# Four row chunks of x at the start of a gated pair of linear-attention blocks: two turned by transposing transfers in place of TensorE, and A's key and query weights loaded from ScalarE's queue

## The chip, the cores and the metric

The kernel runs on 1 core of one Trainium2 chip. The metric is the device time of one execution in microseconds (us), the median over several runs; lower is better.

## What is computed

x is 2048 x 640 (one batch), in bf16. Two linear-attention blocks, A and B, read the same x with their own weights, and a gate mixes their outputs.

```python
def block(x, wqkv, wo):                    # H = 32 heads, Dh = 20
    q, k, v = heads(x @ wqkv)
    phi = lambda t: jnp.where(t > 0, t + 1, jnp.exp(t)) + 1e-6
    pq, pk = phi(q), phi(k)
    kv = jnp.einsum("bhsd,bhse->bhde", pk, v)
    z  = jnp.einsum("bhsd->bhd", pk)
    o  = jnp.einsum("bhqd,bhde->bhqe", pq, kv) / (pq . z + 1e-6)
    return merge(o) @ wo

g = sigmoid((x * gate_w).sum(-1))
out = g * block(x, A_wqkv, A_wo) + (1 - g) * block(x, B_wqkv, B_wo)
```

## The kernel before

**Layout.** Rows of x are worked on in 16 chunks of 128 (four blocks of 512). x is held twice in SBUF: `xn`, rows on the partitions, and `xT`, the 640 columns on the partitions in five pieces `c` of 128. A product x @ W takes a piece of `xT` as the stationary operand and streams W (keys, `kA`, 128 x 320 per half `hf`), or takes W as the stationary operand and streams 512 rows of `xT` (queries, `qA`, `q`). Behind the products ScalarE takes an exponential out of PSUM (`e`) and VectorE clamps it and takes a maximum; results are `pk` (keys) and `pqTA`, `pqTB` (queries). Many of the products are written in a Strassen-like form with sums made on VectorE (`SQ`, `TQ` in `MB` and `TM`). Two hand-written lists of step names, `FIRST` and `PLAN`, set the order of all of that; the change touches neither.

**The start.** The four chunks 0 to 3 (the first 512 rows) come into `xn` by four plain loads (`load_x`, L200): chunks 0 and 1 are called x0 and x1 below. They go through TensorE transposes into PSUM and VectorE copies into `xT` (`x_transpose`, L290 to L296). The other three blocks of 512 rows are turned by 15 transposing transfers on SyncE's queue (L220, 128 columns x 512 rows each). A's key weights `wkA` come in four loads (L203): pieces c = 0, c = 1, c = 2 and c = 3 with 4, called wk0, wk1, wk2 and wk34 here. A's query weights `wqA` come in three (L217): pieces 0 and 1, 2 and 3, and 4, called wq01, wq23 and wq4 here.

TensorE begins with seven warm-up matmuls on constants (`warm`, L252), then turns chunks 0 and 1, and turns the gate's weight vector into a column (`gate_column`, L263 to L268). ScalarE copies that column into `wkA` as its 641st column, in three pieces (L268). Every key matmul of the second half of the columns (`hf` = 1, 321 wide) reads it, so the x @ gate_w sum comes for free. `k_first` (L359) writes out the order of the 40 key matmuls of the chunks 0 to 3, which are 8 (chunks 0 and 1, c = 0 and 1: the four of the first half, then the four of the second), and 32 more with the transposes of the chunks 2 and 3 between them. Then `FIRST` goes on with the first query products (`E.P1` at L753, `sq`/`tq` sums on VectorE, `E.P2`), and the key chunks 4 to 15.

**What orders transfers.** The order of the instructions on each engine is the order of the program text. ScalarE (ACT) and SyncE (SP) each issue transfers on a queue of their own, between their other instructions, and an instruction with a wait holds all that stand behind it on its engine. The tile framework deals out eight completion semaphores to the transfers, one after another in the program's order, both queues together (`DMAHW0` to `DMAHW7`). The ninth transfer takes the semaphore of an earlier one, and waits, on the queue that issues it, until the transfer that had it last has landed. So in the printed instruction order `[waits DMAHW0_49]` on a transfer is a wait for an earlier transfer, often of other data and of the other queue.

Of the kernel before, what the change touches and what calls it, by code (L numbers as in the profile page):

```python
# [9 lines left out]
P = 128  # L10
# [5 lines left out]
S, D, H = 2048, 640, 32  # L16
Dh = D // H
DT = D // P
ST = S // P
NB = 4  # L20
CB = 4
HB = 512
# [56 lines left out]
def kernel(  # L79
# [11 lines left out]
    nc = tc.nc  # L91
    x2 = A_x.flatten_outer_dims()
# [28 lines left out]
    def ps_raw(name, slot=None):  # L121

        if slot is None:
            slot = turn[0]
            turn[0] = (slot + 1) % 4
        return pools.get(slot, pools["ps"]).tile([P, 4 * HB], BF16, tag=f"ps{slot}", name=name)

    def banks(raw):

        return raw.bitcast(FP32).rearrange("p (b n) -> p b n", b=2)  # L130

    def ps(name, slot=None):

        return banks(ps_raw(name, slot))

    xT = persist.tile([P, DT, S], BF16, name="xT")
    xn = persist.tile([P, ST, D], BF16, name="xn")
# [17 lines left out]
    g5 = persist.tile([DT, P], BF16, name="g5")  # L155
# [29 lines left out]
    wq_dram = [A_wqkv.rearrange("(c p) f -> p c f", p=P), B_wqkv.rearrange("(c p) f -> p c f", p=P)]  # L185
# [5 lines left out]
    nc.vector.memset(tiny[:], LOGS * EPS)  # L191
    nc.vector.memset(maskE[:], 1.0)
    nc.vector.memset(E4[0:2 * H, HF:D], 0.0)
    xb0 = x2[0:CB * P, :].rearrange("(p q) d -> p q d", q=CB)
    wk = [None, None]
    wv = [None, None]
    wq = [None, None]
    wk[0] = wpool.tile([P, DT, D + 2], BF16, tag="wk", name="wkA")
    def load_x(eng, lo, hi):
        eng.dma_start(out=xn[:, lo:hi, :], in_=xb0[:, lo:hi, :])  # L200

    def load_wk(eng, lo, hi):
        eng.dma_start(out=wk[0][:, lo:hi, 0:D], in_=wq_dram[0][:, lo:hi, D:2 * D])  # L203

    load_x(nc.sync, 0, 1)
    load_x(nc.scalar, 1, 2)
    load_wk(nc.sync, 0, 1)
    load_wk(nc.scalar, 1, 2)
    nc.sync.dma_start(out=g5[:], in_=gate_w.rearrange("(c p) -> c p", p=P))
    load_x(nc.scalar, 2, 3)  # L210
    load_wk(nc.sync, 2, 3)
    load_x(nc.scalar, 3, 4)
    nc.scalar.preload_act_table_set("natural_log_exp_and_others")
    load_wk(nc.sync, 3, DT)
    wq[0] = wpool.tile([P, DT, D], BF16, tag="wq", name="wqA")
    for lo, hi in ((0, 2), (2, 4), (4, DT)):
        nc.sync.dma_start(out=wq[0][:, lo:hi, :], in_=wq_dram[0][:, lo:hi, 0:D])  # L217
    for n in range(1, NB):
        for c in range(DT):
            nc.sync.dma_start_transpose(  # L220
                out=xT[:, c, n * HB:(n + 1) * HB], in_=x2[n * HB:(n + 1) * HB, c * P:(c + 1) * P]
            )


    make_identity(nc, ident[:])
    for r in range(4):
        rows = slice(32 * r, 32 * r + 32)
        nc.gpsimd.tensor_copy(out=I4[rows], in_=ident[rows, rows])
    nc.gpsimd.tensor_copy(
        out=spread[:].rearrange("p (h t) -> p h t", t=TW), in_=I4[:, :, None].to_broadcast([P, H, TW])  # L230
    )
    for lo in range(0, HF, K6):
        part = maskE[:, lo:min(lo + K6, HF)]
        for sign, base in ((1, 0), (-1, Dh - 1)):
            nc.gpsimd.affine_select(
                out=part, in_=part, pattern=[[-sign * Dh, part.shape[1] // Dh], [0, Dh]],
# [3 lines left out]
    for rows, n in ((slice(0, 2 * H), H // 2), (slice(2 * H, P), H)):  # L240
        nc.gpsimd.tensor_copy(
            out=E4_rows[rows, 0:n], in_=I4[rows, 0:n, None].to_broadcast([rows.stop - rows.start, n, Dh])
# [20 lines left out]
    def gate_column(pt):  # L263

        at = slice(4 * HB - 2 * P, 4 * HB - 2 * P + DT)
        nc.tensor.transpose(out=pt[:, at], in_=g5[:], identity=ident[0:DT, 0:DT])
        for lo, hi in ((0, 1), (1, 2), (2, DT)):
            nc.scalar.copy(out=wk[0][:, lo:hi, D:D + 1], in_=pt[:, at, None][:, lo:hi])  # L268
# [21 lines left out]
    def x_transpose(i, slot):  # L290
        pt = ps_raw("xt", slot)
        for c in range(DT):
            nc.tensor.transpose(out=pt[:, c * P:(c + 1) * P], in_=xn[:, i, c * P:(c + 1) * P], identity=ident[:])
        src = pt[:, 0:D].rearrange("p (c n) -> p c n", c=DT)
        for lo, hi in ((0, 2), (2, DT)):
            nc.vector.tensor_copy(out=xT[:, lo:hi, i * P:(i + 1) * P], in_=src[:, lo:hi])  # L296
# [39 lines left out]
    def k_mm(b, i, c, pt, hf):  # L336
        n = HF + (b == 0 and hf == 1)
        nc.tensor.matmul(  # L338
            pt[:, hf, 0:n], lhsT=xT[:, c, i * P:(i + 1) * P], rhs=wk[b][:, c, hf * HF:hf * HF + n],
            start=(c == 0), stop=(c == DT - 1),  # L340
        )
# [17 lines left out]
    def k_first():  # L359

        pts = []

        def part(i, cs, hfs=(0, 1)):
            for c in cs:
                for hf in hfs:
                    k_mm(0, i, c, pts[i], hf)

        x_transpose(0, 3)
        x_transpose(1, 2)
        gate_column(warm_raw)  # L370
        pts += [ps("kA", 1), ps("kA", 3)]
        for hf in range(2):
            for i in range(2):
                part(i, (0, 1), (hf,))
        x_transpose(2, 0)
        for i in range(2):
            part(i, (2,))
        x_transpose(3, 2)
        pts.append(ps("kA", 0))
        part(2, (0, 1, 2))  # L380
        for i in range(3):
            part(i, (3, 4))
        pts.append(ps("kA", 2))
        for hf in range(2):
            part(3, range(DT), (hf,))
        return pts

    def mixed(t, m):
# [146 lines left out]
    class PhiSteps:  # L535
# [9 lines left out]
        def part(self, t, k):  # L545
            return t if len(self.srcs) == 1 else t[:, k]
# [573 lines left out]
    def rows_of(i):  # L1120
        n, q = divmod(i, CB)
        rows = out2[n * HB:(n + 1) * HB, :]
        return rows.rearrange("(p q) d -> q p d", q=CB)[q] if n == 0 else rows[q * P:(q + 1) * P, :]

    def prod(dst, left, right, i, first, cs=range(DT)):

# [12 lines left out]
    class Pair:  # L1139
# [7 lines left out]
        def store(self, k, lo=0, hi=D):  # L1147
            eng = nc.scalar if self.last and k == 1 else nc.sync
            eng.dma_start(out=rows_of(self.i + k * (ST // 2))[:, lo:hi], in_=self.osb[k][:, lo:hi])
# [163 lines left out]

    with tc.manual_schedule():
        pts = k_first()
        for n in range(1, NB):
            nc.sync.dma_start(
                out=xn[:, n * CB:(n + 1) * CB, :], in_=x2[n * HB:(n + 1) * HB, :].rearrange("(q p) d -> p q d", p=P)
            )
# [3 lines left out]
        lo, hi = GT  # L1323
# [197 lines left out]
        part = [slice(n * RB, (n + 1) * RB) for n in range(4)]  # L1521
# [70 lines left out]
        for i in range(1, half):  # L1592
            p, after = pairs[i], pairs[i + 1] if i + 1 < half else None
# [7 lines left out]
            q = after if i + 2 < half else p if after is None else None  # L1601
# [42 lines left out]
```

## Time and profile before

| what | value |
|---|---|
| median of 3 runs | 181.88 us (181.76 to 182.73) |
| the profiled execution, its own time | 182.31 us |
| its span in the profile | 180.5 us |
| busy: TensorE, VectorE, ScalarE | 176.9, 152.0, 112.0 us |
| transposing transfers on SyncE's queue | 15, issued from 5.80 us on |
| first query matmul (L753) | 11.64 us |

The profiled execution's own time is 1.8 us over its span, which is what lies around the span, and 0.43 us over the median of the runs. Times in the profile count from the start of the span. In the rows of the timeline the first number is a start, the second the length to the end of the last instruction of a merged group; "x8" is how many were merged; brackets give idle time ahead of it and what ended that. ACTq and SPq are the issuing of transfers by ScalarE and SyncE; PE is TensorE's matmuls, PEld its weight loads, DVE VectorE.

### The profile page before, as it was taken

The page shows a single profiled execution, that of the slowest core. Times are in us where ns is not written, and L with a number is a line of the kernel's source. Part 1 is how long each engine was busy: PE and PEld are TensorE (multiplying, and loading weights), DVE is VectorE, ACT ScalarE, POOL GpSimd, SP SyncE. Part 2 cuts the span into 40 slices and gives each one's busy share as a digit, 9 for nine tenths or more (in the row PEclk, how much of TensorE's full clock was granted, in tenths as well). Part 3 has the DMA queues.
Part 4 walks back from the last instruction along what each step waited for, and adds up shares of the span by engine and source line. Part 5 has one row for each costly group of instructions (what it writes and reads, how often), then busy time and mean ns, then how long its engine had stood idle before and what let it go on. Part 6 is the DMA issues. An engine that isn't in the chain of part 4 may idle for free.

```text
span 180.5 us, 3397 instructions
## 1 busy us (share of the span) xinstructions
PE 176.9 (98%) x1276; PEld 117.6 (65%) x1276; DVE 152.0 (84%) x287; ACT 112.0 (62%) x235; POOL 4.4 (2%) x19
## 2 busy tenths in 40 slices
PE   8999999999999999999999999999999999999993
PEld 3666666665666677666656676766678777777772
DVE  1479999999999996888899997987988988686774
ACT  2098988999763434587778686774815756456410
POOL 7100000000000000000000000000000000000000
PEclk9999999999999999999999999999999999999999
DMA  5995449976035015000000024144901560133123
GB/s 184 284 187 91 97 106 291 356 158 182 0 112 185 8 54 181 2 0 0 2 4 2 0 32 153 31 127 123 264 3 48 167 153 0 40 137 119 73 101 120
DMA packets 21602, 18.85 MB, mean 104 GB/s; under 512 B 9298, under 2 KB 21074, under 8 KB 21586
## 3 DMA queue, kind: packets, MB, share of 16 engines
q1 hardware_dynamic: 20722, 17.82, 35.3%
q10 hardware_dynamic: 864, 0.82, 1.3%
q8 instruction: 10, 0.16, 0.4%
q14 instruction: 6, 0.05, 0.1%
HBM read 11.86 MB, written 4.80 MB: 92 GB/s over the span
## 4 chain that ended last, share of the span: by engine, by line
PE 96%; ACT 2%; DVE 1%; issue 0%
PE q L527 16%; PE kA L338 11%; PE kB L338 9%; PE gs L845 9%; PE gs L1333 9%; PE oy L1129 6%; PE oz L1129 5%; PE ox L1129 5%; PE ow L1129 4%; PE kB L527 3%; PE qA L393 3%; PE gB L815 2%; PE gA L815 2%; PE warm L252 2%; ACT e L551 1%; PE q L393 1%
## 5 line engine op out<-in xcount | busy, mean ns | idle before, releaser
L338 PEld LDWEIGHTS <-xT 128*128 128x128 bf16 x280 | 27.3, 98 | 15.1 <-DVE xT L296 0.2
L338 PE MATMUL kA<-wkA,xT 128*128 128x320 bf16 (+1 forms) x160 | 24.8, 304 | 0.0
L551 ACT ACTIVATE e<-q 128x512 bf16<-128x512 f32 x32 | 18.5, 599 | 5.7 <-PE q L527 5.2
L557 DVE TENSOR_SCALAR e<-e 128x640 bf16<-128x640 bf16 (+2 forms) x59 | 19.0, 334 | 2.9 <-ACT e L551 2.6
L338 PE MATMUL kB<-wkB,xT 128*128 128x320 bf16 x120 | 19.2, 299 | 0.0
L551 ACT ACTIVATE e<-kB 128x640 bf16<-128x640 f32 (+1 forms) x18 | 11.4, 647 | 7.3 <-PE kB L527 3.2
L551 ACT ACTIVATE e<-kA 128x640 bf16<-128x640 f32 x16 | 11.4, 720 | 5.8 <-PE kA L338 5.2
L533 DVE TENSOR_TENSOR q<-q,p 128x512 f32<-128x512 f32 x16 | 11.1, 695 | 1.7 <-PE q L527 1.2
L564 DVE SCALAR_TENSOR_TENSOR pk<-kB,e 128x640 bf16<-128x640 f32 (+1 forms) x16 | 11.6, 735 | 0.4
L1129 PEld LDWEIGHTS <-xT 128*128 128x128 bf16 x85 | 8.1, 98 | 2.9
L1129 PEld LDWEIGHTS <-pqTA 128*128 128x128 bf16 x85 | 8.1, 98 | 2.8
L1192 ACT COPY u<-ox 128x320 f32<-128x320 f32 x8 | 3.4, 425 | 10.4 <-PE ox L1129 10.4
L1129 PEld LDWEIGHTS <-pqTB 128*128 128x128 bf16 x80 | 7.8, 98 | 3.0
L527 PE MATMUL q<-xT,wqB 128*128 128x512 bf16 x32 | 9.7, 379 | 0.0
L1134 DVE TENSOR_TENSOR osb<-oz,u 128x320 bf16<-128x320 f32 (+2 forms) x18 | 7.9, 452 | 1.9 <-PE oz L1129 1.6
L527 PE MATMUL q<-SQ,TM 128*128 128x512 bf16 x32 | 8.5, 379 | 0.0
L1333 PEld LDWEIGHTS <-xn 128*128 128x128 bf16 x64 | 6.1, 98 | 3.1 <-issue 0.7
L815 PEld LDWEIGHTS <-xn 128*128 128x128 bf16 x64 | 6.3, 98 | 2.8
L845 PEld LDWEIGHTS <-xn 128*128 128x128 bf16 x64 | 6.1, 98 | 2.9 <-issue 0.7
L564 DVE SCALAR_TENSOR_TENSOR pk<-kA,e 128x640 bf16<-128x640 f32 x8 | 6.5, 818 | 0.4 <-DVE e L557 0.2
L564 DVE SCALAR_TENSOR_TENSOR pqTB<-q,e 128x512 bf16<-128x512 f32 x10 | 6.7, 682 | 0.0
L1129 PE MATMUL oz<-MB,xT 128*128 128x320 bf16 (+2 forms) x45 | 6.8, 284 | 0.0
(205 smaller groups left out, 376.3 us busy)
## 6 DMA issues: line engine op xcount, KB each, us to landing
out_dram<-osb SPq DMA_DIRECT2D x14, 160.0 KB, 1.8
xn<-in_A_x_dram SPq DMA_DIRECT2D x3, 640.0 KB, 5.8
wvA<-in_A_wqkv_dram SPq DMA_DIRECT2D x1, 800.0 KB, 9.1
wkB<-in_B_wqkv_dram SPq DMA_DIRECT2D x1, 800.0 KB, 4.5
wqB<-in_B_wqkv_dram SPq DMA_DIRECT2D x1, 800.0 KB, 7.1
wvB<-in_B_wqkv_dram SPq DMA_DIRECT2D x1, 800.0 KB
MA<-m_rows SPq DMA_DIRECT2D x1, 800.0 KB, 5.1
MB<-m_rows SPq DMA_DIRECT2D x2, 400.0 KB, 4.1
```

Source lines behind the costliest of these rows:

```text
L338: nc.tensor.matmul(pt[:, hf, 0:n], lhsT=xT[:, c, i * P:(i + 1) * P], rhs=wk[b][:, c, hf * HF:hf * HF + n], start=(c == 0), stop=(c == DT - 1),
L393: nc.tensor.matmul(dst, lhsT=mixed(wq[b][:, c, :], m), rhs=xT[:, c, n * HB:(n + 1) * HB], start=first, stop=last,)
L527: nc.tensor.matmul(dst, lhsT=left(c), rhs=right(c), start=first and k == 0, stop=last and k == len(cs) - 1, skip_group_check=not first,)
L533: nc.vector.tensor_tensor(out=dst, in0=acc, in1=sb, op=ALU.add)
L551: nc.scalar.activation(out=self.part(self.e, k), in_=self.srcs[k](), func=ACT.Exp)
L557: nc.vector.tensor_scalar(self.e, self.e, 1.0, EPS, op0=ALU.min, op1=ALU.add)
L564: nc.vector.scalar_tensor_tensor(out=self.part(self.dst, k), in0=src(), scalar=1.0 + EPS, in1=self.part(self.e, k), op0=ALU.add, op1=ALU.max,)
L815: nc.tensor.matmul(pt[:, hf, 0:HF], lhsT=xn[:, i, c * P:(c + 1) * P], rhs=pk[:, i, hf * HF:(hf + 1) * HF], start=(i == 0), stop=(i == ST - 1),
L845: nc.tensor.matmul(pt[:, n, 0:HF], lhsT=left[:, i, n * P:(n + 1) * P], rhs=right[:, i, :], start=(first and i == 0), stop=(i == hc - 1), s ...
L1129: nc.tensor.matmul(dst, lhsT=left[:, c, r0:r0 + P], rhs=right[:, c, :], start=(first and c == 0), stop=(c == DT - 1), skip_group_check=not ...
L1134: nc.vector.tensor_tensor(out=dst, in0=acc, in1=sb, op=ALU.add)
L1333: nc.tensor.matmul(dst[n], lhsT=left[:, i, n * P:(n + 1) * P], rhs=right[:, i, :], start=(first and i == 0), stop=(i == hc - 1), skip_grou ...
```

## The change

Chunks 2 and 3 no longer pass through TensorE: `load_xT(256, 512)` turns them by five transposing transfers, 128 columns x 256 rows, issued second on SyncE's queue. `k_first` loses `x_transpose(2, 0)` and `x_transpose(3, 2)` with their 10 TensorE transposes and 4 VectorE copies, and takes the key matmuls in another order. The plain rows of chunks 2 and 3 are loaded later, in one load behind all transposing transfers. All of `wkA`, the gate's weights and all of `wqA` are issued by ScalarE, ahead of its first computing instruction. The first 512 rows are taken in natural order (row = 128 q + p) where they were interleaved (row = 4 p + q), both in the load and in the store.

```diff
-    xb0 = x2[0:CB * P, :].rearrange("(p q) d -> p q d", q=CB)
+    xb0 = x2[0:CB * P, :].rearrange("(q p) d -> p q d", p=P)
+    def load_xT(lo, hi):
+        for c in range(DT):
+            nc.sync.dma_start_transpose(out=xT[:, c, lo:hi], in_=x2[lo:hi, c * P:(c + 1) * P])
+
     load_x(nc.sync, 0, 1)
     load_x(nc.scalar, 1, 2)
-    load_wk(nc.sync, 0, 1)
+    load_wk(nc.scalar, 0, 1)
+    load_xT(HB // 2, HB)
+    nc.scalar.dma_start(out=g5[:], in_=gate_w.rearrange("(c p) -> c p", p=P))
     load_wk(nc.scalar, 1, 2)
-    nc.sync.dma_start(out=g5[:], in_=gate_w.rearrange("(c p) -> c p", p=P))
-    load_x(nc.scalar, 2, 3)
-    load_wk(nc.sync, 2, 3)
-    load_x(nc.scalar, 3, 4)
+    load_wk(nc.scalar, 2, 3)
     nc.scalar.preload_act_table_set("natural_log_exp_and_others")
-    load_wk(nc.sync, 3, DT)
+    load_wk(nc.scalar, 3, DT)
     wq[0] = wpool.tile([P, DT, D], BF16, tag="wq", name="wqA")
     for lo, hi in ((0, 2), (2, 4), (4, DT)):
-        nc.sync.dma_start(out=wq[0][:, lo:hi, :], in_=wq_dram[0][:, lo:hi, 0:D])
+        nc.scalar.dma_start(out=wq[0][:, lo:hi, :], in_=wq_dram[0][:, lo:hi, 0:D])
     for n in range(1, NB):
-        for c in range(DT):
-            nc.sync.dma_start_transpose(
-                out=xT[:, c, n * HB:(n + 1) * HB], in_=x2[n * HB:(n + 1) * HB, c * P:(c + 1) * P]
-            )
+        load_xT(n * HB, (n + 1) * HB)
...
-        x_transpose(2, 0)
-        for i in range(2):
-            part(i, (2,))
-        x_transpose(3, 2)
-        pts.append(ps("kA", 0))
-        part(2, (0, 1, 2))
-        for i in range(3):
-            part(i, (3, 4))
-        pts.append(ps("kA", 2))
-        for hf in range(2):
-            part(3, range(DT), (hf,))
+        for c in range(2, DT):
+            for i in range(2):
+                part(i, (c,))
+        pts += [ps("kA", 0), ps("kA", 2)]
+        for i in range(2, CB):
+            part(i, range(DT))
...
-        return rows.rearrange("(p q) d -> q p d", q=CB)[q] if n == 0 else rows[q * P:(q + 1) * P, :]
+        return rows[q * P:(q + 1) * P, :]
...
         pts = k_first()
+        nc.sync.dma_start(out=xn[:, 2:CB, :], in_=xb0[:, 2:CB, :])
```

On ScalarE's queue, from its first instruction on, the program before has these rows. L200 loads x1, then chunks 2 and 3; L203 is wk1; `warm` holds the gate's column; the last row is the first exponential of the keys.

```order
L200 DMA xn<-in_A_x_dram 128x640
L203 DMA wkA<-in_A_wqkv_dram 128x640
L200 DMA xn<-in_A_x_dram 128x640 x2
L213 ACT_TABLE_LOAD
L268 COPY wkA<-warm 128x1 [waits PE_49]
L268 COPY wkA<-warm 128x1
L268 COPY wkA<-warm 128x3
L551 ACTIVATE e<-kA 128x640 [waits PE_49]
```

The changed program has, at the same place (`g_89` is the gate's weights; L203 is wk0, wk1, wk2, wk34 in this order, L220 is wq01, wq23, wq4):

```order
L200 DMA xn<-in_A_x_dram 128x640
L203 DMA wkA<-in_A_wqkv_dram 128x640
L213 DMA g_89<-in_gate_w_dram 5x128
L203 DMA wkA<-in_A_wqkv_dram 128x640 [waits DMAHW1_49]
L203 DMA wkA<-in_A_wqkv_dram 128x640 [waits DMAHW3_49]
L216 ACT_TABLE_LOAD
L203 DMA wkA<-in_A_wqkv_dram 128x2x640 [waits DMAHW0_49]
L220 DMA wqA<-in_A_wqkv_dram 128x2x640 [waits DMAHW4_49]
L220 DMA wqA<-in_A_wqkv_dram 128x2x640 [waits DMAHW7_49]
L220 DMA wqA<-in_A_wqkv_dram 128x640 [waits DMAHW2_49]
L268 COPY wkA<-warm 128x1 [waits PE_49]
```

Six transfers with waits for other transfers now stand ahead of the gate's copies (L268); there were none.

On SyncE's queue the program before begins so (x0, wk0, the gate's weights, wk2, wk34, the three loads of `wqA`, and the first of 15 transposing transfers):

```order
L200 DMA xn<-in_A_x_dram 128x640
L203 DMA wkA<-in_A_wqkv_dram 128x640
L209 DMA g_89<-in_gate_w_dram 5x128
L203 DMA wkA<-in_A_wqkv_dram 128x640
L203 DMA wkA<-in_A_wqkv_dram 128x2x640 [waits DMAHW0_49]
L217 DMA wqA<-in_A_wqkv_dram 128x2x640 [waits DMAHW1_49]
L217 DMA wqA<-in_A_wqkv_dram 128x2x640 [waits DMAHW2_49]
L217 DMA wqA<-in_A_wqkv_dram 128x640 [waits DMAHW3_49]
L220 DMA_TRANSPOSE xT<-in_A_x_dram 128x512 [waits DMAHW4_49]
```

The changed program begins so. The transposing transfers are called T0 to T19 below, in the order of the queue: T0 to T4 are the new ones (256 rows), T5 to T19 the 15 that were there (512 rows). The last row here is T11.

```order
L200 DMA xn<-in_A_x_dram 128x640
L207 DMA_TRANSPOSE xT<-in_A_x_dram 128x256 x4
L207 DMA_TRANSPOSE xT<-in_A_x_dram 128x256 [waits DMAHW0_49]
L207 DMA_TRANSPOSE xT<-in_A_x_dram 128x512 [waits DMAHW2_49]
L207 DMA_TRANSPOSE xT<-in_A_x_dram 128x512 [waits DMAHW4_49]
L207 DMA_TRANSPOSE xT<-in_A_x_dram 128x512 [waits DMAHW5_49]
L207 DMA_TRANSPOSE xT<-in_A_x_dram 128x512 [waits DMAHW6_49]
L207 DMA_TRANSPOSE xT<-in_A_x_dram 128x512 [waits DMAHW7_49]
L207 DMA_TRANSPOSE xT<-in_A_x_dram 128x512 [waits DMAHW1_49]
L207 DMA_TRANSPOSE xT<-in_A_x_dram 128x512 [waits DMAHW2_49]
```

The weights have gone from this queue, and the transposing transfers have moved up to its second place. In the changed program the semaphores are held in this order: 0 by x1, then T4, then wk34; 1 by x0, then wk1; 2 by wk0, T5, T11, wq4; 3 by T0, then wk2; 4 by T1, T6, wq01; 5 by T2, T7; 6 by the gate's weights, T8; 7 by T3, T9, wq23. So ScalarE's transfers wait for these: wk1 for x0, wk2 for T0, wk34 for T4, wq01 for T6, wq23 for T9, and wq4 for T11.

## The prediction

> **What bounds the kernel now.** I read the page's busy line and chain first.
>
> ```profile
> PE 176.9 (98%) x1276; PEld 117.6 (65%) x1276; DVE 152.0 (84%) x287; ACT 112.0 (62%) x235; POOL 4.4 (2%) x19
> PE 96%; ACT 2%; DVE 1%; issue 0%
> ```
>
> TensorE is busy for 98% of the span and carries 96% of the chain that ended last. So a delay of TensorE at one place goes to the end unless a later idle time swallows it. The view by stretches, cut where the first query matmul begins, shows how little there is to swallow it.
>
> ```profile
> 0.00:11.64 11.64, 10.80 (x69) 6.68 (x69) 4.18 (x17) 3.84 (x11) 4.42 (x19) 1.00 0.93 227
> 11.64:180.50 168.86, 166.06 (x1210) 110.88 (x1207) 147.85 (x272) 108.20 (x225) 0.00 (x0) 1.00 0.33 96
> ```
>
> The columns are the stretch's length and the busy times of PE, PEld, DVE, ACT and POOL, then the granted clock, the DMA share and GB/s. Behind 11.64 us TensorE idles 2.8 of 168.9 us in all. The waits of its weight loads name no transfer there, so later transfers have no say, and the question is only when TensorE comes to the first query matmul. The timeline of the start says what happens until then.
>
> ```profile
> 0.84 2.93 PE L252 MATMUL warm<-const-bfloat16-1.0 128*128 128x512 bf16 x7 [0.84 <-PEq L1628]
> 4.93 1.93 PE L338 MATMUL kA<-wkA,xT 128*128 128x320 bf16 x8
> 5.04 0.30 ACT L268 COPY wkA<-warm 128x1 bf16<-128x1 bf16 x3 [1.05 <-PE warm L266]
> 6.70 0.44 PE L293 MATMUL xt<-ident,xn 128*128 128x128 bf16 x5
> 7.53 0.44 PE L293 MATMUL xt<-ident,xn 128*128 128x128 bf16 x5
> 7.80 4.00 PE L338 MATMUL kA<-wkA,xT 128*128 128x320 bf16 x28
> 11.64 1.03 PE L753 MATMUL qA<-xT,wqA 128*128 128x512 bf16 x4
> 12.68 1.27 PE L393 MATMUL qA<-xT,wqA 128*128 128x512 bf16 x5
> ```
>
> TensorE gets through it nearly without a gap. The two groups of five transposes at 6.70 and 7.53 us are those that the change takes out. The gate's copies (L268) run at 5.04 us, just ahead of the first 321-wide matmul, which needs them.
>
> **The waits that the change adds.** The changed program puts six loads with semaphore waits ahead of the gate's copies on ScalarE. What such a wait does, the queue waits and the timeline of SyncE show before the change.
>
> ```profile
> SPq L203 <- DMA xn<-in_A_x_dram: 1.3, 1, 1.3
> xn<-in_A_x_dram ACTq DMA_DIRECT2D x1, 160.0 KB, 3.0
> 0.80 0.41 ACTq L200 DMA_DIRECT2D xn<-in_A_x_dram  x1
> 3.81 0.39 SPq L203 DMA_DIRECT2D wkA<-in_A_wqkv_dram  x1
> 4.25 1.49 SPq L217 DMA_DIRECT2D wqA<-in_A_wqkv_dram  x3
> ```
>
> The load of wk34 reads nothing of `xn`, yet it stood 1.3 us until x1, issued by the other engine at 0.80, had landed 3.0 us later, and went out at 3.81. That is semaphore 0 being reused. The three loads of `wqA` stood behind it. On the Trainium skill's "DMA: Bandwidth & Descriptors" (Anatomy of one DMA), transfers themselves wait for no semaphore and the issuing sequencer does; the trace agrees by these 1.3 us.
>
> So the gate's copies come when ScalarE has issued wq4, which waits for T11, the twelfth transposing transfer on SyncE. When does T11 land?
>
> ```profile
> L220 SPq DMA_TRANSPOSE xT<-in_A_x_dram x15: 1223/1259/1887, 5.8 to 24.7; - x15
> DMA to landing us min/median/max: 2.8/2.9/5.8
> 7.07 2.65 SPq L220 DMA_TRANSPOSE xT<-in_A_x_dram  x2
> 14.98 1.89 SPq L220 DMA_TRANSPOSE xT<-in_A_x_dram  x1
> xT<-in_A_x_dram SPq DMA_TRANSPOSE x2, 3.6
> 1.26 0.42 SPq L203 DMA_DIRECT2D wkA<-in_A_wqkv_dram  x1
> L200 SPq DMA_DIRECT2D xn<-in_A_x_dram x1: 393/393/393, 0.8 to 0.8; - x1
> ```
>
> A transposing transfer of 512 rows takes SyncE 1.26 us to issue. From 7.07 to 14.98 us six went out, so one each 1.32 us. One of 256 rows has no row. It lies between a plain load's 0.39 us and the full 1.26; I take the middle, 0.83, a period of 0.87 with the gap to the next. T0 starts where the queue's second instruction starts now, at 1.26. T4 follows four periods later at 4.74, behind x1's landing at 3.80, so its own wait costs nothing. T5 starts at 5.61 and T11 six full periods on, at 13.5. Its own waits and those of T6 to T10 are for transfers issued 4 us and more ahead, and the landings here are 2.9 in the median. T11 lands at 16.4.
>
> Bounds of this: 256 rows for a plain load's 0.39 (T4 then waits for x1 until 3.80, and T11 lands at 15.0), and 256 rows as dear as 512, a landing of 3.6 (as of the pair at 14 us) and the one long issue of 1.89 falling ahead of T11 (it lands at 20.0).
>
> ```profile
> L217 SPq DMA_DIRECT2D wqA<-in_A_wqkv_dram x3: 465/467/469, 4.3 to 5.3; - x3
> L268 ACT COPY wkA<-warm x3: 163/169/192, 5.0 to 5.1; 128x1 bf16<-128x1 bf16 x2, 128x3 bf16<-128x3 bf16 x1
> 5.97 0.89 PE L338 MATMUL kA<-wkA,xT 128*128 128x321 bf16 x4
> ```
>
> Issuing wq4 takes 0.47 us and the first copy 0.17, so the fifth key matmul (the first 321 wide) starts at about **17.1 us** where it now starts at 5.97 (bounds 15.6 and 20.6). Four key matmuls run before it. The late loads of wk1, wk2 and wk34 (each behind x0, T0 and T4, which land by 8 us) are hidden under this stall, and so are wq01 and wq23; each alone would stop TensorE for some us if the copies were not held.
>
> **What goes away, and what comes back.**
>
> ```profile
> L338 PE MATMUL kA<-wkA,xT 128*128 128x320 bf16 (+1 forms) x160 | 24.8, 304 | 0.0
> 5.17 1.01 PE L338 MATMUL kA<-wkA,xT 128*128 128x320 bf16 x3
> 5.44 1.01 PE L338 MATMUL kA<-wkA,xT 128*128 128x320 bf16 x3
> 6.97 0.71 PE L338 MATMUL kA<-wkA,xT 128*128 128x320 bf16 x4
> 12.67 0.80 PEld L393 LDWEIGHTS <-wqA 128*128 128x128 bf16 x5 [0.48 <-DVE pk L564]
> ```
>
> The remaining 36 key matmuls follow each other in 0.137 us (28 in 4.00 us, less the last one's 0.30, over 27), 4.9 us. Before, the same stretch from 5.97 to 11.64 took 5.7, so the ten transposes give back 0.7. The VectorE copies that go lie beside TensorE and give nothing.
>
> The starts at 5.17 and 5.44 are 0.27 us apart, twice the later 0.137: TensorE runs its first stretch at half pace, although the granted clock reads 1.00. The change of pace lies between 5.97 and 6.97, some 5.6 us behind the first warm-up matmul at 0.84. After 10 us of idling I expect that stretch once more: 5.6 us at half pace lose 5.6 x (1 - 0.137/0.267) = 2.7 us. The trace has no long gap, so zero is the other end; I take 2.7, as the only row of a start after idling has it. On the Trainium skill's "TensorE: Matmul & The Clock Gate" (Part 1: The HAM clock gate), an idle window of about 3.4 us takes the array to half clock and 3.4 us of sustained work brings it back. By that the term would be an estimated 1.7, and the sum 1.0 us less; the half pace of the start agrees, the gap is what no row shows.
>
> At L393 the weight load waited 0.48 us for VectorE's `pk`. Four query matmuls at 0.22 us (five in 1.27, with the last one's 0.38) from 11.64 would have ended at 12.5, so the wait cost 0.2. In the new order chunk 0 is complete 22 matmuls ahead of the queries instead of 18 and this wait goes. Natural row order moves rows of the same 1,280 B, at nothing. The late load of the plain rows of chunks 2 and 3 stands with the other plain rows behind the last transposing transfer, and its first reader, VectorE's sum S, comes at 35.9 us:
>
> ```profile
> L1065 DVE TENSOR_TENSOR S<-xn x2: 681/682/683, 35.9 to 41.8; 128x1024 bf16<-128x1024 bf16 x2
> 26.04 2.32 SPq L1317 DMA_DIRECT2D xn<-in_A_x_dram  x3
> ```
>
> SyncE comes to these loads at about 25 us by the same count (8 more periods from T11, at 24.1, and then the load), so TensorE's delay gives them slack. Without that slack their lateness would be under 1 us.
>
> **Sum.** 11.1 (17.1 less 5.97) - 0.7 (transposes) + 2.7 (half pace) - 0.2 (L393) = **+12.9 us**. The span goes from 180.5 to 193.4, the profiled execution's own time from 182.31 to 195.2; it stood 0.4 over the median of the runs, so for the median of 181.88 I predict **194.8 us**.
>
> **Rivals.** *The restart is at full pace* (no half-pace stretch): 12.9 - 2.7 = +10.2, 192.1 us. For it, the granted clock is 1.00 in every stretch; against it, so it is at the start too, where the pace was half. Chance 0.16.
>
> *A waiting load on ScalarE doesn't hold what stands behind it*, or the copies come through in time. Then wq4 itself is the bound: issued at 16.4 to 16.9, landing 3.3 us later (the 160 KB wk1 on ScalarE's queue), at 19.7, for the fifth matmul of L393, which starts at 13.6 now.
>
> ```profile
> wkA<-in_A_wqkv_dram ACTq DMA_DIRECT2D x1, 160.0 KB, 3.3
> ```
>
> That is +6.1 us, 188.0. Against it stands SyncE's row at 3.81: the loads behind did wait. Chance 0.08.
>
> *The waits are off the path*, and the change is a gain: the place is the gate's copies, the price the 0.7 and 0.2 above, 181.0 us, and it decides at 5.97 us: T11 would have to land by about 5.3, so be issued by 2.4, twelve transposing transfers in 1.2 us where one takes 1.26. On the Trainium skill's "DMA: Bandwidth & Descriptors" (Issuing engines are not separate DMA queues), issuing from another engine changes only the sequencer's issue time, which would give this case; the row of 1.3 us of waiting speaks against it. Chance 0.03.
>
> **How the numbers follow.** The forecast has 0.70, the full-pace restart 0.16, the unheld copies 0.08, the gain 0.03; the rest is for still longer stalls. The range takes in the first two with their bounds: from 192.1 less 1.5 (copies at 15.6), 190.6, to 194.8 plus 3.5 (copies at 20.6), 198.3. It leaves out less than 2 in 10. Faster by over 0.5%, which is about what a measurement of this kernel can tell from no change, has 0.03; within 0.5%, 0.01; slower 0.96.
>
> **What the profile after would show.** ScalarE's queue has loads of `wkA` and `wqA` strung out to 16 or 17 us, with the copies L268 behind them; TensorE has four key matmuls near 5 to 7 us, then a gap of some 10 us that ends on L268; then key matmuls 0.27 us apart for 3 to 6 us. The new transposing transfers take 0.6 to 1.1 us of SyncE each. Behind the first query matmul, at about 24.7 us, all runs as before, 13 us later. I'm wrong if L268 runs before 10 us, if the gap ends on something else, or if later stages win the time back.

## The result and the profile after

The changed kernel takes **197.5 us** (median of 4 runs, 197.31 to 198.35); the kernel before, on the same chip, 182.11 (4 runs, 181.76 to 182.73). The ratio is 1.085, with a 95% interval of 1.0804 to 1.0896: slower. The profiled execution took 197.31 us with a span of 195.6, against 182.31 and 180.5, so 15.0 us of time and 15.1 of span are to be explained.

First the busy line, the chain that ended last and the costliest group of key matmuls, from the page after.

```profile
PE 178.0 (91%) x1256; PEld 117.9 (60%) x1266; DVE 151.1 (77%) x283; ACT 112.5 (58%) x235; POOL 4.4 (2%) x19
PE 88%; SPq 7%; DMA 2%; issue 1%; DVE 1%; ACTq 0%; ACT 0%
L338 PE MATMUL kA<-wkA,xT 128*128 128x320 bf16 (+1 forms) x160 | 26.8, 320 | 13.0 <-ACT wkA L268 12.2
```

TensorE has the same work but for the ten transposes, yet is busy for 91% of the span, not 98%. SyncE's queue, which was not on the chain, now holds 7% of it. The key matmuls stood idle for 13.0 us where it was 0.0, and 12.2 of that ended on ScalarE's copy of the gate's column. TensorE's timeline after shows the place.

```profile
6.13 0.96 PE L338 MATMUL kA<-wkA,xT 128*128 128x320 bf16 x3 [0.79 <-DMA wkA<-in_A_wqkv_dram]
19.30 7.21 PE L338 MATMUL kA<-wkA,xT 128*128 128x321 bf16 x36 [12.21 <-ACT wkA L268]
26.34 1.03 PE L748 MATMUL qA<-xT,wqA 128*128 128x512 bf16 x3
27.20 1.24 PE L388 MATMUL qA<-xT,wqA 128*128 128x512 bf16 x5
```

The first key matmul (at 4.89) and three more run, TensorE stands for 12.2 us, and the other 36 follow in one piece. The first query matmul comes at 26.34 in place of 11.64, the second group at 27.20 in place of 12.68. ScalarE's timeline after says why the copies are late; x2 and x3 are groups of loads with the waits between them.

```profile
3.47 1.72 ACTq L203 DMA_DIRECT2D wkA<-in_A_wqkv_dram  x2
8.81 0.39 ACTq L203 DMA_DIRECT2D wkA<-in_A_wqkv_dram  x1
12.66 6.38 ACTq L220 DMA_DIRECT2D wqA<-in_A_wqkv_dram  x3
19.08 0.30 ACT L268 COPY wkA<-warm 128x1 bf16<-128x1 bf16 x3 [12.58 <-DMA xT<-in_A_x_dram]
```

The loads are strung out: wk1 and wk2 from 3.47, wk34 at 8.81, the three of `wqA` from 12.66 to 19.04. ScalarE's 12.58 us of waiting ahead of the copies are put down to a transposing transfer, which the copies do not read. The chain that ended last names the transfer; here is its piece from T4 on (start, length).

```profile
6.36 1.24 SPq L207
...
7.65 1.26 SPq L207
...
15.47 3.20 DMA xT<-in_A_x_dram
...
18.69 0.35 ACTq L220
...
19.08 0.17 ACT wkA L268
```

The chain runs through SyncE's issuing of one transposing transfer after the other until T11, which is issued at 15.47 and lands 3.20 us later. At that moment ScalarE issues wq4, and then the copies run. Behind the first query matmul nothing is won back or lost:

```profile
26.34:195.60 169.26, 165.49 (x1200) 110.93 (x1207) 147.58 (x270) 108.32 (x225) 0.00 (x0) 1.00 0.30 89
```

That stretch is 169.3 us long, 0.4 more than the 168.9 before, and the 0.4 lies behind the last computation, which ends 14.65 us later than before (192.69 against 178.04). All else happened ahead of 26.34 us.

### The profile page after: what moved, and what is told of

Its sections match the earlier page's. It is cut to its first block, busy times and chain, and to the rows that moved or that the text cites. A ratio compares the mean times of both kernels' runs of the same rounds, so it can differ in the third digit from the quotient of the medians.

```text
span 195.6 us, 3365 instructions
## 1 busy us (share of the span) xinstructions
PE 178.0 (91%) x1256; PEld 117.9 (60%) x1266; DVE 151.1 (77%) x283; ACT 112.5 (58%) x235; POOL 4.4 (2%) x19
## 4 chain that ended last, share of the span: by engine, by line
PE 88%; SPq 7%; DMA 2%; issue 1%; DVE 1%; ACTq 0%; ACT 0%
PE q L522 14%; PE kA L338 12%; PE kB L338 9%; PE gs L840 8%; PE gs L1329 8%; SPq L207 7%; PE oy L1124 6%; PE oz L1124 5%; PE ox L1124 4%; PE ow L1124 4%; PE kB L522 2%; PE gB L810 2%; PE gA L810 2%; PE qA L388 2%; DMA xT<-in_A_x_dram 2%; PE q L388 1%
## 5 line engine op out<-in xcount | busy, mean ns | idle before, releaser
L338 PEld LDWEIGHTS <-xT 128*128 128x128 bf16 x280 | 28.2, 101 | 29.9 <-issue 12.8
L338 PE MATMUL kA<-wkA,xT 128*128 128x320 bf16 (+1 forms) x160 | 26.8, 320 | 13.0 <-ACT wkA L268 12.2
L528 DVE TENSOR_TENSOR q<-q,p 128x512 f32<-128x512 f32 x16 | 11.1, 696 | 1.7 <-PE q L522 1.2
L1124 PEld LDWEIGHTS <-xT 128*128 128x128 bf16 x85 | 8.1, 98 | 2.9
L268 ACT COPY wkA<-warm 128x1 bf16<-128x1 bf16 (+1 forms) x3 | 0.3, 174 | 12.6 <-DMA xT<-in_A_x_dram 12.6
```

What stands on the lines that cost most here:

```text
L338: nc.tensor.matmul(pt[:, hf, 0:n], lhsT=xT[:, c, i * P:(i + 1) * P], rhs=wk[b][:, c, hf * HF:hf * HF + n], start=(c == 0), stop=(c == DT - 1),
L528: nc.vector.tensor_tensor(out=dst, in0=acc, in1=sb, op=ALU.add)
L1124: nc.tensor.matmul(dst, lhsT=left[:, c, r0:r0 + P], rhs=right[:, c, :], start=(first and c == 0), stop=(c == DT - 1), skip_group_check=not ...
```

## The experiments

Eleven kernels were run beside those two. The edits are given against the changed kernel, except where the text says before.

### Two semaphores fewer: one_wq

```diff
-    for lo, hi in ((0, 2), (2, 4), (4, DT)):
-        nc.scalar.dma_start(out=wq[0][:, lo:hi, :], in_=wq_dram[0][:, lo:hi, 0:D])
+    nc.scalar.dma_start(out=wq[0][:], in_=wq_dram[0][:, :, 0:D])
```

> The changed kernel with A's query weights in one load instead of three, still on ScalarE at the same place. Two semaphores fewer are dealt, so the one load waits for T6 (as wq01 does in the change, where it went out at 12.66 us) and not for T11; the bytes, the engines and the rest of the order are the same. Theory (the copies come when the query weight loads have found a free semaphore): copies at 13.1 us in place of 19.1, the gap of TensorE is 6 us shorter, the 36 key matmuls still begin at half pace (7 us), the first query matmul comes at about 20.3 us in place of 26.3, and the time is 191.3 us (190.3 to 192.3). Rival (what ScalarE waits for isn't the dealt semaphore but the transfers ahead on its queue or the DMA engines): copies still at 18 us or later, 196 us or more.

Measured: 191.59 us (191.36 to 191.93), ratio 1.052 (1.0505 to 1.0536). T6 on the chain that ended last, then ScalarE and TensorE in this kernel:

```profile
8.94 4.57 DMA xT<-in_A_x_dram
...
13.53 0.40 ACTq L219 DMA_DIRECT2D wqA<-in_A_wqkv_dram  x1
13.97 0.30 ACT L267 COPY wkA<-warm 128x1 bf16<-128x1 bf16 x3 [7.12 <-DMA xT<-in_A_x_dram]
14.18 6.89 PE L337 MATMUL kA<-wkA,xT 128*128 128x321 bf16 x36 [7.45 <-ACT wkA L267]
```

The same bytes come over the same queue, the one load is larger than any it replaces, and yet ScalarE is free 5.1 us earlier. What it waited for was the semaphore and not the transfers ahead of it, and the rival is out: T6 lands at 13.51, the load goes out at 13.53. That is 0.9 us later than reckoned (12.66, as wq01 in the change), because T6, issued at the same time in both (8.94 and 8.95), takes 4.57 us to land here.

### The query weights back on SyncE: wq_sync

```diff
-        nc.scalar.dma_start(out=wq[0][:, lo:hi, :], in_=wq_dram[0][:, lo:hi, 0:D])
+        load_wq(nc.sync, lo, hi)
```

`load_wq` is the same `dma_start`, with the engine as an argument.

> The changed kernel with one edit: the three loads of A's query weights go back to SyncE's queue, behind the five new transposing transfers; A's key weights and the gate's weights stay on ScalarE. Theory (ScalarE is held by the query weight loads, which wait for late transposing transfers): wk34 now waits only for the gate's weights, so it goes out behind the table load at about 6.5 us and lands near 9.7; the gate's copies run at about 7 us instead of 19.1, the first query matmul comes at 13 to 14.5 us instead of 27, and the time is about 185 us (184 to 186.5). Rival (the twenty transposing transfers themselves are what is late, whoever issues the weights): the copies come early but TensorE still waits on xT, and the time stays above 190 us.

Measured: 184.81 us (184.47 to 185.02), ratio 1.0129 (1.0109 to 1.0149). So 12.7 of the 15.4 us between the medians hang on which engine issues three loads. What is left (2.4 us over the 182.43 that the kernel before took beside it) is seen in these rows (copies, key matmuls, first query matmul):

```profile
6.73 0.30 ACT L271 COPY wkA<-warm 128x1 bf16<-128x1 bf16 x3
9.01 4.01 PE L341 MATMUL kA<-wkA,xT 128*128 128x320 bf16 x28 [0.67 <-DMA wkA<-in_A_wqkv_dram]
12.86 1.03 PE L751 MATMUL qA<-xT,wqA 128*128 128x512 bf16 x3
```

TensorE comes to the first queries 1.2 us later than before and to the second group 1.0 (13.72 against 12.68). The rest falls later. TensorE's weight loads wait three times for `xT`, 1.0 us in all. And the plain rows of x now go out behind 20 transposing transfers, at 30.7 us in place of 26.0, and VectorE's S waits for them (queue rows of SyncE, then the wait). Of these 1.3 us some 0.5 reach TensorE: its key matmuls just before come 1.66 us later than in the kernel before (39.07 against 37.41), the query matmuls behind them 2.18 (40.96 against 38.78), and the last computation 2.2.

```profile
30.67 2.25 SPq L1316 DMA_DIRECT2D xn<-in_A_x_dram  x3
```

```profile
DVE S L1063 <- DMA xn<-in_A_x_dram: 1.3, 1, 1.3
```

### TensorE kept busy through the gap: warm_gap

```diff
+            if hf == 1:
+                fill = banks(ps_raw("fill", 2))
+                for _ in range(52):
+                    nc.tensor.matmul(fill[:, 0, 0:HB], lhsT=one_l, rhs=one_r[:, 0:HB], start=True, stop=True)
```

> The changed kernel with 52 more matmuls on constants, 512 wide, between the fourth and the fifth key matmul: they fill the 12 us in which TensorE idles for the gate's copies, in another PSUM slot, and are read by nothing. Theory (TensorE runs at half pace for some us behind a long idle time, although the granted clock reads 1.00): the 36 key matmuls behind the copies run at full pace from the first, 4.9 us in place of 7.04, so the time falls by 2.1 us, to about 195.4. Rival (those matmuls are slow for another reason, say the transfers that land beside them, or the fill comes too late): no change, 197.5 us.

Measured: 195.35 us (194.81 to 195.5), ratio 1.0703 (1.0681 to 1.0725), 2.15 us under the change. TensorE in this kernel (one of the 52 is missing from the record):

```profile
6.49 11.54 PE L376 MATMUL fill<-const-bfloat16-1.0 128*128 128x512 bf16 x51
19.46 5.11 PE L338 MATMUL kA<-wkA,xT 128*128 128x321 bf16 x36 [1.43 <-ACT wkA L268]
24.41 1.03 PE L752 MATMUL qA<-xT,wqA 128*128 128x512 bf16 x3
```

The copies come as late as in the change, but the 36 matmuls take 4.95 us to the first query matmul (24.41 less 19.46), not 7.04. The slow restart is TensorE's own, from idling, and worth 2.1 us. The transfers beside it are not its cause.

### The copies on VectorE: gate_dve

```diff
-            nc.scalar.copy(out=wk[0][:, lo:hi, D:D + 1], in_=pt[:, at, None][:, lo:hi])
+            nc.vector.tensor_copy(out=wk[0][:, lo:hi, D:D + 1], in_=pt[:, at, None][:, lo:hi])
```

> The changed kernel with the gate's three copies into wkA on VectorE instead of ScalarE, all else the same. Theory (the copies are held behind ScalarE's waiting loads): the copies run at about 5.5 us, TensorE goes on to c = 2 at 8 us and is then stopped by wk34 (issued at 8.8, landing at 12.0); what ends last becomes wq4 (issued at 18.7, landing at 23.0) for the fifth matmul of L388, which ran at 28.1 in the changed kernel; so 5 us faster than the changed kernel, 192.4 us (191.5 to 193.5). Rival (the copies are only the messenger: TensorE would have stopped as long for weights or for turned x): the copies run early, TensorE still restarts at 19 us or later, 197 us. Second rival (a load that waits holds only the loads behind it): ScalarE's exponentials come before 19 us; by the theory the first is at 19.05, behind wq4.

Measured: 194.28 us (192.72 to 195.52), ratio 1.0676 (1.06 to 1.0752). Only 3.2 us come back, where 5 were expected. The profiled execution is the fastest of the four, 192.72 us. TensorE in it:

```profile
13.09 5.94 PE L338 MATMUL kA<-wkA,xT 128*128 128x320 bf16 x28 [3.01 <-DMA wkA<-in_A_wqkv_dram]
```

Then ScalarE with the three query weight loads and the first exponential, and TensorE's first query matmul:

```profile
13.52 5.77 ACTq L220 DMA_DIRECT2D wqA<-in_A_wqkv_dram  x3
19.34 0.70 ACT L546 ACTIVATE e<-kA 128x640 bf16<-128x640 f32 x1 [11.93 <-PE kA L338]
21.43 1.02 PE L748 MATMUL qA<-xT,wqA 128*128 128x512 bf16 x3 [2.40 <-DVE pk L559]
```

The copies run at 5.62 on VectorE, and the next two things that the same queue holds take their place: wk34, for which TensorE waits 3.0 us, and then the first exponential of the keys, which stands behind wq4 on ScalarE. The profile puts its 11.93 us of idling down to TensorE's `kA`, but those products were there some 4 us before (the eighth matmul of the group, at 0.267 us each, comes at about 15.2); it starts as soon as the last load has gone out (the group of three began at 13.52 and ended at 19.29). Through `pk` it stops TensorE for another 2.4 us. So a load that waits holds ScalarE's computing too, as the theory had it. What it left out is that the products need the exponentials, and that TensorE is slow behind its wait (28 matmuls in 5.94 us, which take 4.00 at full pace).

### Each half of the change alone: turn and queues

`turn` takes the five transposing transfers and leaves the weights on the queues they had, with `wqA` behind T4:

```diff
-    load_wk(nc.scalar, 0, 1)
+    load_wk(nc.sync, 0, 1)
...
+    load_xT(HB // 2, HB)
...
-        nc.scalar.dma_start(out=wq[0][:, lo:hi, :], in_=wq_dram[0][:, lo:hi, 0:D])
+        nc.sync.dma_start(out=wq[0][:, lo:hi, :], in_=wq_dram[0][:, lo:hi, 0:D])
```

> The other part alone: chunks 2 and 3 turned by five transposing transfers and the key matmuls in the new order, but the weights on the queues as before the change (wk1 on ScalarE, the others on SyncE, wqA behind the five new transfers). No load stands ahead of the gate's copies with a wait. Theory: no long gap at the copies (they run at about 5 us); what costs is SyncE's time, five more issues of 1.28 us: T4 lands at about 11, wqA is issued from 9.4 us and lands at 13 to 14, the first query matmul at about 13, chunk 4's turned pieces at 14 to 19; so about 3 us slower than before, 184.8 us (183.5 to 186.5). Rival (the turned transfers are the main cost of the change): 190 us or more.

Measured: 186.26 us (186.22 to 186.59), ratio 1.0217 (1.0171 to 1.0263). SyncE's queue in it, and the waits of key weight loads and matmuls on `xT`:

```profile
2.99 6.33 SPq L207 DMA_TRANSPOSE xT<-in_A_x_dram  x5
11.01 20.31 SPq L207 DMA_TRANSPOSE xT<-in_A_x_dram  x15
```

```profile
PEld L338 <- DMA xT<-in_A_x_dram: 5.1, 6, 1.3
PE kA L338 <- DMA xT<-in_A_x_dram: 3.1, 4, 0.9
```

Five more issues cost SyncE 6.3 us, and the other 15 begin at 11.0 in place of 5.8. TensorE then waits for `xT`, 3.1 us in all, which it never did before.

`queues` is the kernel before (chunks 2 and 3 turned by TensorE) with all key, gate and query weights on ScalarE as in the change, and chunks 2 and 3 loaded by SyncE:

```diff
-    load_wk(nc.sync, 0, 1)
+    load_wk(nc.scalar, 0, 1)
+    load_x(nc.sync, 2, 3)
+    load_x(nc.sync, 3, 4)
...
-        nc.sync.dma_start(out=wq[0][:, lo:hi, :], in_=wq_dram[0][:, lo:hi, 0:D])
+        nc.scalar.dma_start(out=wq[0][:, lo:hi, :], in_=wq_dram[0][:, lo:hi, 0:D])
```

> One part alone: the kernel before, with chunks 2 and 3 still turned on TensorE and their loads on SyncE, but all of wkA, the gate's weights and all of wqA issued by ScalarE ahead of the gate's copies, as in the change. wq4 now shares its semaphore with the seventh transposing transfer (issued at about 10, landing at about 13). Theory: copies at about 13.6 us, TensorE's gap ends there, some 2 us of half pace behind it, first query matmul at about 21.5, 191.8 us (189.5 to 193). Rival (turning chunks 2 and 3 by transfers is what costs, through late xT or contention): no gap of more than 2 us, 182 to 184 us.

Measured: 193.25 us (192.96 to 194.13), ratio 1.0605 (1.0551 to 1.0659):

```profile
14.64 0.30 ACT L268 COPY wkA<-warm 128x1 bf16<-128x1 bf16 x3 [9.26 <-DMA xT<-in_A_x_dram]
14.86 1.23 PE L338 MATMUL kA<-wkA,xT 128*128 128x321 bf16 x4 [8.03 <-ACT wkA L268]
```

The queue move alone does harm of the same kind without one added transposing transfer: the 15 old ones are enough. The time is 0.25 us above the range that was expected, with the copies at 14.64 us, not 13.6. The two halves cost 4.2 and 11.2 us over the 182.08 us that the kernel before took beside them, 15.4 together, as much as the whole. That they add up is in part chance: `turn` pays with TensorE's waits for `xT`, of which the change has none; there wq4 instead waits for a later transfer than in `queues`, and the copies come at 19.08 in place of 14.64.

### Row order alone: natural

The kernel before with only the first 512 rows in natural order, in loads and store.

> The kernel before with only the row order changed: the first 512 rows natural (row = 128 q + p), in the four loads and in the store. Theory (rows of the same 1,280 B, at nothing): ratio 1.000, within 0.995 to 1.005. Rival (loads or stores of scattered rows cost or save at an end of the kernel): outside that.

Measured: 182.16 us (12 runs, 181.57 to 182.72), ratio 0.9996 (0.9984 to 1.0008). Nothing.

### Four attempts to beat both kernels

All four keep the turning by transfer, take ScalarE's waits on late transfers away, and take the keys of chunks 2 and 3 by column pieces. None beats the kernel before. Their loads, T being the rows of the groups of five transposing transfers:

```diff
 best:       wk0, wk2, wk34 on ScalarE, wk1 on SyncE; g and wqA (3 loads) on GpSimd; T 768, 1024
 wide_1024:  wk0, g, wk2, wk34, wqA (1 load) on ScalarE, wk1 on SyncE; T 1024, 512, 256
 early_256:  as wide_1024, g on GpSimd; T 256, 512, 512, 512
 lean_turn:  wk0, wk2, wk34 on ScalarE, wk1 on SyncE, g on GpSimd; T 256, wqA (1 load) behind it, T 1024, 512
```

> A version without the waits: rows 256 to 1023 of each column piece turned by one transfer of 768 rows (five of these), rows 1024 to 2047 by one of 1024 rows (five), so 10 issues where the change has 20; wk0, wk2, wk34 on ScalarE with no wait, wk1 on SyncE, the gate's weights and wqA on GpSimd's queue. If an issue's cost hardly depends on the rows (1.21 to 1.25 us for 256, 1.26 for 512), the 768 and 1024 ones take 1.3 us and T4 lands at about 10.5: first query matmul at about 11, 181.3 us (180.5 to 182.5). If it grows with the rows beyond 512 (0.5 us or more per 256 rows), T4 lands at 13 or later and it is 184 or more. GpSimd's issue times are in no row so far.

Measured: 194.4 us (191.26 to 194.85). The four runs lie 3.6 us apart, so no ratio is given, and only the transfers are read. DMA queue rows of the stretch 1 to 8 us:

```profile
wkA<-in_A_wqkv_dram ACTq DMA_DIRECT2D x1, 320.0 KB, 14.6
xT<-in_A_x_dram SPq DMA_TRANSPOSE x3, 16.4
```

Transposing transfers of 768 rows beside the weight loads landed 16.4 us after issue, and wk34 14.6. I had counted the issue time alone, and taken the landing from before.

> An attempt to beat both kernels: chunks 2 and 3 by transposing transfers, but of 1024 rows (rows 256 to 1279) five times, then 512 rows five times and 256 rows five times, so that SyncE issues them at about 1.3 us each; wk1 on SyncE, the other key weights, the gate's weights and A's query weights as one load on ScalarE, ahead of its computing; keys of chunks 2 and 3 in order of the column pieces. On ScalarE the semaphore waits are then only for x1 and wk0. Theory (only the waits on ScalarE and late transfers cost): the copies run at 5 to 6 us, the first query matmul comes at 11.0 to 12.5 us, and the time is 181 to 183 us. Rival (the transfers are short of the DMA engines: before, they are busy for 93% of the first 11.64 us at 227 GB/s, and here 0.65 MB more fall into that stretch, 2.9 us): about 185 us.

Measured: 190.68 us (190.07 to 191.38), ratio 1.0455 (1.0418 to 1.0492). Two stretches and TensorE's longest group; in the stretches the last three numbers are granted clock, DMA share and GB/s.

```profile
4.00:8.00 4.00, 2.00 (x18) 1.27 (x16) 1.02 (x4) 1.58 (x4) 1.33 (x4) 0.92 1.16 136
8.00:12.00 4.00, 1.83 (x7) 0.72 (x6) 0.00 (x0) 0.00 (x0) 0.00 (x0) 0.50 1.17 173
```

```profile
12.91 6.27 PE L340 MATMUL kA<-wkA,xT 128*128 128x320 bf16 x28 [1.79 <-DMA wkA<-in_A_wqkv_dram]
```

The DMA engines are full (a share of 1.16) while they move 136 GB/s. The weights that share them are late: wk34, issued at 3.53, lands 9.34 us later, where the kernel before has 4.3. TensorE waits (1.8 us for the gate's weights, then 1.3 and 1.8 for `wkA`), its clock falls to half between the first and the second of these waits, and the 28 matmuls take 6.3 us in place of 4.0. The rival named the cause, though its 185 us left out the clock.

> As wide_1024, but the five new transposing transfers have 256 rows as in the change and the others 512, and the gate's weights are on GpSimd's queue. ScalarE's waits are for x1 and wk2. Theory: the copies run at 5 to 6 us and the new transfers go out from 1.7 to 8 us; the next five start at about 8 us, against 5.8 before and 11.0 in the kernel with only the turning changed (186.3 us), so TensorE waits a little for rows 512 to 1023: about 183 us (181.5 to 184.5). Rival (the queries wait for the one large query weight load or for the DMA engines): 185 us or more.

Measured: 185.5 us (184.24 to 186.32), ratio 1.0162 (1.0116 to 1.0209). ScalarE, then TensorE:

```profile
6.12 0.43 ACTq L211 DMA_DIRECT2D wqA<-in_A_wqkv_dram  x1
7.87 0.30 ACT L270 COPY wkA<-warm 128x1 bf16<-128x1 bf16 x3
8.09 4.00 PE L340 MATMUL kA<-wkA,xT 128*128 128x321 bf16 x28 [1.83 <-ACT wkA L270]
```

Even a wait of 2 us for wk2's landing puts the copies, behind `wqA` and the table load, 2.8 us later than before, and TensorE stands for 1.8 of them. The time is the rival's, its reason is not: TensorE waits for no load of `wqA` here.

> A last attempt to turn chunks 2 and 3 by transfer without losing: five transposing transfers of 256 rows behind x0 and wk1 on SyncE, A's query weights as one load behind them, then rows 512 to 1535 by five of 1024 rows and the rest by five of 512, so that SyncE issues 15 transposing transfers as before; wk0, wk2 and wk34 on ScalarE (one wait, for x1), the gate's weights on GpSimd's queue; keys of chunks 2 and 3 in order of the column pieces. Theory (what is left is the five more issues of 1.25 us on SyncE ahead of rows 512 and up, and the DMA engines in the first 12 us): the copies run at 5.5 us, the first query matmul at 12 to 13 us, and the plain rows come early enough again, so 183.3 us (182 to 185). Rival (the transfers are free when nothing waits for semaphores): at or under 181.8 us. Rival (transfers of 1024 rows occupy the DMA engines beside the plain load): 186 us or more.

Measured: 186.24 us (186.11 to 187.89), ratio 1.0244 (1.0212 to 1.0275). The copies run at 5.54 as meant, and then:

```profile
13.31 1.06 PE L751 MATMUL qA<-xT,wqA 128*128 128x512 bf16 x4 [1.53 <-DMA wqA<-in_A_wqkv_dram]
18.57 0.45 PE L340 MATMUL kA<-wkA,xT 128*128 128x320 bf16 x2 [0.74 <-DMA xT<-in_A_x_dram]
```

`wqA` and rows 512 to 1023 come too late, because five issues of 1.25 us stand ahead of them; one of the five issues of 1024 rows took 2.95 us besides. The time is again that of a rival (186 us or more), its reason is not: `wqA` lands 5.1 us after issue, no later than the 5.4 to 5.8 of its loads in the kernel before, but is issued at 8.11 in place of 4.25. What turning by transfer can bring is the 0.7 and 0.2 us of the prediction. None of the six kernels without long waits on ScalarE ahead of the copies (these four, `turn` and `wq_sync`) got them back: the added transfers cost more, on SyncE's queue or on the DMA engines.

## Why the prediction was right, and what it mis-sized

The mechanism stood: 194.8 us was predicted, 197.5 measured, within the range. Of the 2.7 us between them 2.1 lie in the kernel; the other 0.6 is that the profiled execution stood 0.4 over the median before and 0.2 under it after. By the prediction's own steps:

**TensorE's delay goes to the end: right.** The second query group is 14.5 us late (27.20 against 12.68) and the last computation 14.65. The span has 0.45 us more, behind the last computation, where the last store lands later; no run isolates that, so it stays open.

**A reused semaphore holds ScalarE until T11 has landed: right, and shown** by `one_wq`, where fewer transfers mean an earlier partner, and by `wq_sync`, where the waits are on another engine. One sentence on the kernel before is to be corrected: the framework deals the semaphores not quite in the program's order. In the change x1 has semaphore 0 and x0, written ahead of it, semaphore 1; the table looks like the order in which the framework reckons the transfers to go out, which no run tests. The table of holders was read from the printed waits and stands.

**When T11 lands: mis-sized, the largest error.** The step took 0.83 us for issuing 256 rows, as the middle between a plain load and 512 rows. It is 1.21 to 1.25 (T4's row at 6.36 above: 1.24), as dear as 512. T5 went out at 7.65, not 5.61, and T11 at 15.47, not 13.5: +2.0. It landed 3.20 us after issue, not 2.9: +0.3. wq4's issue took 0.35, not 0.47: -0.1. So the fifth key matmul came at 19.30, not 17.1, +13.3 in place of +11.1. The upper bound had said "as dear as 512"; no row spoke for the middle.

**The ten transposes, 0.7: right.** At full pace the 36 matmuls take 4.95 us (`warm_gap`) where 4.9 was worked out and 5.7 stood before.

**The restart at half pace: right in kind, too long.** It was put at 2.7 us, from 5.6 us of half pace at the kernel's start. It is 2.1 (7.04 less 4.95), 4.3 us of half pace. Counts of matmuls in three stretches of 2 us of the change show it end:

```profile
19.30:21.30 2.00, 2.00 (x8) 1.16 (x8) 0.00 (x0) 0.08 (x2) 0.00 (x0) 1.00 1.12 199
21.30:23.30 2.00, 2.00 (x10) 1.09 (x8) 0.00 (x0) 0.06 (x1) 0.00 (x0) 1.00 1.34 150
23.30:25.30 2.00, 2.00 (x15) 1.40 (x14) 1.17 (x3) 1.50 (x5) 0.00 (x0) 1.00 0.60 120
```

8, then 10, then 15 matmuls. The start was a poor model for its length: the 5.6 us were counted from the first warm-up matmul, and nothing showed from when the clock counts. No one length would have served: where the clock is on record, it came back 2.7 to 4.9 us into the work behind a gap (last section). The estimate of 1.7 us from the Trainium skill's "TensorE: Matmul & The Clock Gate" (Part 1: The HAM clock gate) is 0.4 low, as 2.7 is 0.6 high.

**The wait at L393, -0.2: right** (the second query group follows the first by 0.86 us in place of 1.04). **Natural row order, nothing: right** (`natural`).

**The late plain rows: right here, under-sized in general.** In the change S waits for nothing, because TensorE's own delay covers it. "Under 1 us" without that cover was too low for VectorE, which waits 1.3 us in `wq_sync`; some 0.5 of them reach TensorE.

**Sum.** +13.3 - 0.7 + 2.1 - 0.2 = +14.5 at the second query group, +0.1 to the last computation, +0.45 behind it: +15.1 of span. The late landing missed by +2.2 and the restart by -0.6; with the +0.5 behind the second query group, which the prediction did not have, 2.1 remain. That the last two cancel is luck.

**The rivals.** The full-pace restart is refuted (`warm_gap`). The case of copies that are not held was priced at 188.0, with wq4's landing as the bound. `gate_dve` made it, and it took 194.3: the price left out wk34's own wait, the slow pace behind it, and that the exponentials stand on the same engine behind the same loads. The gain, for which the Trainium skill's "DMA: Bandwidth & Descriptors" (Issuing engines are not separate DMA queues) was named, is refuted as far as it rests on issue time: it says that another issuing engine changes the sequencer's issue time only. As to the transfers that may be so; here the engine that issues also computes, and `wq_sync` puts 12.7 us on it.

## What to carry to other kernels

Don't put a transfer that has to wait for a free semaphore ahead of computing on the engine that issues it; count the transfers in flight against the semaphores, and read the waits of the printed order as "waits until that transfer lands". On a queue that only issues, such a wait costs what stands behind it; on ScalarE it also costs every product that needs ScalarE. And where a term has two bounds and no row between them, ask which of its parts scale with size before taking the middle.

## What the hardware showed that was not expected

**Issuing a transposing transfer costs the same for 256, 512 and 1024 rows of 128 columns when nothing holds it up**: 1.21 to 1.25, 1.26, and 1.26 us (the first of `wide_1024`). Halving such transfers does not make them cheaper for the queue. The next four of 1024 rows in `wide_1024`, with the DMA engines full, took 2.0 to 5.2 us each; why was not tested.

**Transposing transfers beside plain loads fill the DMA engines at a low rate.** A share of 1.16 at 136 GB/s in `wide_1024`; before, the first 11.64 us had a share of 0.93 at 227 GB/s. It does not take 1024 rows: the change, with 512, has 1.34 at 150 GB/s from 21.30 to 23.30 us.

**The granted clock can read 1.00 at half pace.** In the change's profiled execution it reads 1.00 in the three stretches above, though TensorE goes through 8 matmuls in the first and 15 in the third. Another of its four runs, 198.35 us, has a mean clock of 0.955 over its span, which is some 17.7 us at half, about the gap and the slow stretch together (16.5); the other three read 0.997 to 1.00. In `one_wq`, behind a shorter gap, the profile has it:

```profile
5.00:7.00 2.00, 0.95 (x5) 0.46 (x6) 0.52 (x3) 1.28 (x1) 0.40 (x1) 1.00 0.75 189
7.00:8.00 1.00, 0.00 (x0) 0.00 (x0) 0.00 (x0) 0.00 (x0) 0.00 (x0) 0.82 0.38 90
8.00:12.00 4.00, 0.00 (x0) 0.00 (x0) 0.00 (x0) 0.00 (x0) 0.00 (x0) 0.50 0.57 141
16.00:17.90 1.90, 1.90 (x9) 1.07 (x8) 0.00 (x0) 0.00 (x0) 0.00 (x0) 0.51 1.08 355
17.90:20.90 3.00, 3.00 (x23) 2.15 (x22) 1.81 (x5) 2.59 (x7) 0.00 (x0) 1.00 0.90 195
```

The clock falls to half between 7 and 8 us, 0.9 us behind the end of the fourth key matmul at 6.74 (a mean of 0.82 over that microsecond puts the fall at 7.64), and is full again at 17.9, 3.7 us after work began anew. In `queues` the same reading puts the fall at 7.29 and the return at 17.53, 2.7 us after work began anew at 14.86:

```profile
7.00:7.50 0.50, 0.00 (x0) 0.00 (x0) 0.00 (x0) 0.00 (x0) 0.00 (x0) 0.79 1.24 268
7.50:17.50 10.00, 2.64 (x14) 1.71 (x14) 0.56 (x2) 0.30 (x3) 0.00 (x0) 0.50 1.00 217
17.50:18.00 0.50, 0.50 (x8) 0.46 (x7) 0.01 (x1) 0.00 (x0) 0.00 (x0) 0.97 0.82 74
```

`wide_1024` (7.38 to 17.62) and `best` (11.48 to 21.72, 4.9 us after work began anew at 16.86) have such a stretch too. All four last 10.2 us, whenever the work began within them. So the return does not come a fixed time of work after the restart: the 2.7 to 4.9 us lie on both sides of the 3.4 us of sustained work that the Trainium skill's "TensorE: Matmul & The Clock Gate" (Part 1: The HAM clock gate) gives. The Trainium skill's page also says that its window of 3.4 us runs free of the work. The 10.2 us are three times that and agree with it, though no run was made to test it.

The fall in `one_wq` comes sooner than a wholly idle window of that length would allow: TensorE was busy for 0.95 of the 2 us up to 7.00, so a window with some work in it sufficed. What share of work keeps the clock up was not measured: `early_256` idled for 1.83 us and went on at full pace in its profiled execution.
